# Softmax sums of a fused attention and feed-forward kernel: from TensorE to VectorE, with the transposes moved

## The chip, the cores and the metric

The kernel runs on one core of one Trainium2 chip. The metric is the device time of one execution in microseconds (us). Every experiment ran on the same chip as, and in turn with, the kernel before.

## The reference

Attention with normalised queries and keys, then a feed-forward layer with a squared ReLU, all in float32:

```python
q, k, v: (8, 12, 448, 64)          # batch, heads, sequence, head size
q_n = q / sqrt(mean(q*q, -1) + 1e-6) * g_q        # the same for k
attn = softmax(q_n @ k_n.T / 8)                   # 448 x 448 for each head
x = (attn @ v), rearranged to (3584, 768)
out = square(maximum(x @ w_in, 0)) @ w_out        # 768 -> 2048 -> 768
```

## The kernel before

Two heads make a pair, and there are 48 pairs. Twelve pairs make a span, and for each of the four spans a first product (`w_in`) and a second product (`w_out`) follow, each as seven block products in place of eight. The first twelve pairs run alone at the start. The other 36 are woven, twelve at a time, into the second product of spans 0 to 2. I call these three stretches the **stages**. In a stage TensorE alternates between a piece of second product (`ps`) and a piece of attention. The profiles show each matmul of the code as two records (`values()` issues eight for a pair, the trace has `pav` x16); counts of matmuls below are of records, save the 12.1 a pair in the prediction.

A pair of the stages, as `attention()` issued it before (each `yield` lets a piece of the second product in; cuts are marked):

```python
def attention(work, first):
    last = first + 2 * NPAIR
    for i in range(first, last + 1):
        if i + 3 < min(last + 2, B * NPAIR):
            load(i + 3)                    # q, k through SyncE's queue
        if i < last:
            scores(i, 0); scores(i, 1)     # TensorE sc, then ScalarE exp -> pr
        if i == first:
            yield
        if i > first:
            values(i - 1, False)           # TensorE pav (16), tot (4)
        if i < last:
            add_up(work, i, 1)             # VectorE acc = pr0 + pr1
            scores(i, 2); scores(i, 3)
        if i > first:
            finish(i - 1)                  # VectorE xT = pav * (1 / tot)
        yield
        if i < last:
            add_up(work, i, 2); add_up(work, i, 3)
        ...                                # combine_x(i - 1), load_v(i + 1)
        yield
        if i + 1 < last:
            transposes(i + 1)              # VectorE qk -> qkT
        if i + 2 < last:
            norm(i + 2)
        yield
```

The parts that matter below (line numbers in the profiles are of the kernel that was run: `acc` is L761 before and L760 after):

```python
def norm_by_squares(i):
    nc.scalar.activation(qkn..., raw..., AF.Square)                    # L707
    nc.vector.tensor_reduce(half, ..., AX, ALU.add)                    # L710
    ...                                                # L713 to L715, small
    nc.gpsimd.tensor_tensor(half, half, mhalf, ALU.pow)                # L716, 128x28
    for s in range(2):
        nc.gpsimd.tensor_tensor(qkn[:, s], raw[:, s], half..., ALU.mult)   # L718
    normed[i] = qkn

def transposes(i):
    ...
    for s in range(2):
        nc.vector.transpose(qkT[:, 0, s], qkn[:, s]...)                # L728
    nc.scalar.activation(qkT[:, 0, 0], qkT[:, 0, 0], AF.Copy, scale=gains[:, 0:1])   # L729

def values(i, pe_sums):
    pavs[i] = ps_o.tile([P, S], F32, tag="o", name="pav")              # one buffer in PSUM
    ...                                                                # 16 records
    sums(i, accs.pop(i), True, True)       # 4 records, with ones: sum over the keys, on all 64 rows

def finish(i):
    ...
    nc.vector.reciprocal(x, tot)           # 128x448
    nc.vector.tensor_tensor(x, pav, x, ALU.mult)
```

## Time and profile before

| | before |
|---|---|
| time, median | 1441.1 us (1440.99 to 1442.78, 3 runs) |
| profiled span | 1439.2 us |
| GpSimd's power L716, 36 times | mean 4813 ns |
| ScalarE's copy of qkT, waiting for VectorE's transposes | 174.0 us in all |
| VectorE's first sum, waiting for TensorE's tot | 122.3 us in all |

The busy shares, the stages and one pair's beat (the time from one pair to the next on TensorE) are shown in the prediction. In the profiles PE is TensorE, PEld its weight loads, DVE VectorE, ACT ScalarE, POOL GpSimd and SP SyncE; a q behind the name (SPq, ACTq) marks an instruction that issues a transfer. I cut the span at points of equal work: the first matmul of the first second product, then, in each stage, the start of the last 34 matmul records of the second product, which nothing interrupts. Stretch 1 is thus the start, 2 the first stage, 3 and 4 a first product and a stage each, and 5 the last products. This is the view of busy times by stretch; after the stretch and its length come PE, PEld, DVE, ACT and POOL busy with their instructions, the mean granted clock, the DMA share and GB/s.

```profile
0.00:275.43 275.43, 262.32 (x1022) 117.66 (x1022) 209.00 (x259) 200.78 (x307) 206.25 (x169) 0.99 0.79 252
275.43:479.21 203.78, 202.22 (x729) 87.13 (x727) 147.04 (x217) 58.55 (x73) 67.91 (x30) 1.00 0.46 98
479.21:822.68 343.47, 343.33 (x1106) 157.77 (x1105) 187.50 (x285) 83.28 (x115) 114.64 (x68) 1.00 0.41 97
822.68:1166.04 343.36, 343.24 (x1106) 157.78 (x1105) 188.18 (x285) 83.19 (x115) 113.79 (x68) 1.00 0.39 94
1166.04:1439.20 273.16, 265.53 (x706) 134.01 (x706) 72.64 (x117) 24.03 (x43) 31.52 (x32) 0.99 0.37 94
```

Subtract the second number from the first to read TensorE's idle time: 1.56 us in the first stage, 0.14 and 0.12 in the next two.

### The profile page before, as it was taken

How to read it: one execution, taken by the hardware profiler on the slowest of the kernel's cores; microseconds unless marked ns; L12 is line 12 of the kernel's file. 1: busy time of each engine (PE TensorE's matmuls, PEld its weight loads, DVE VectorE, ACT ScalarE, POOL GpSimd, SP SyncE). 2: the span in 40 equal slices, each digit the busy share in tenths (PEclk: the TensorE clock that was granted, in tenths of full speed). 3: DMA queues.
4: the chain of work that ended last, by engine and by line, in shares of the span. 5: the costliest groups of instructions: out<-in, count | busy, mean ns of one | idle time of the engine just before them, and what ended most of it. 6: DMA issues, size and time to landing. Idle time of an engine off the chain costs nothing.

```text
span 1439.2 us, 14368 instructions
## 1 busy us (share of the span) xinstructions
PE 1416.6 (98%) x4662; PEld 654.4 (45%) x4662; DVE 804.4 (56%) x1163; ACT 449.8 (31%) x652; POOL 534.1 (37%) x367
## 2 busy tenths in 40 slices
PE   7999999999999999999999999999999999999997
PEld 3433454444444455444444455544444445555553
DVE  6778888478767433456666633355666652332111
ACT  6887687423323012133232111223323201110000
POOL 5877688333442022523444012433334302221000
PEclk9999999999999999999999999999999999999999
DMA  8576898644445333344454342343544333333443
GB/s 236 171 219 162 301 383 315 180 87 107 101 89 102 97 88 88 97 98 106 98 109 88 89 102 87 93 115 81 109 98 103 76 83 87 87 88 102 106 113 70
DMA packets 423639, 180.37 MB, mean 125 GB/s; under 512 B 274820, under 2 KB 421508, under 8 KB 423556
## 3 DMA queue, kind: packets, MB, share of 16 engines
q1 hardware_dynamic: 419716, 178.91, 47.4%
q10 hardware_dynamic: 3712, 0.46, 0.2%
q8 instruction: 39, 0.64, 0.2%
q14 instruction: 44, 0.36, 0.1%
q0 software_dynamic: 128, 0.00, 0.0%
HBM read 146.28 MB, written 33.03 MB: 125 GB/s over the span
## 4 chain that ended last, share of the span: by engine, by line
PE 92%; DVE 4%; DMA 2%; issue 1%; ACT 1%; POOL 0%; SPq 0%; DVEq 0%; POOLq 0%; ACTq 0%
PE ps L973 32%; PE sc L748 11%; PE pav L772 10%; PE pd L926 10%; PE pa L926 10%; PE pc L926 10%; PE pb L926 5%; PE tot L783 4%; DVE acc L761 1%; DVE xT L796 1%; DMA sw<-w1s 1%; PE pt L734 1%; DMA words<-in_moe_w_out_dram 0%; ACT qkT L729 0%; DMA vt<-in_v_dram 0%
## 5 line engine op out<-in xcount | busy, mean ns | idle before, releaser
L716 POOL TENSOR_TENSOR half<-half,mhalf 128x28 f32<-128x28 f32 x36 | 173.3, 4813 | 343.1 <-DVE half L715 343.1
L973 PE MATMUL ps<-gT,sw 128*128 128x448 f32 x768 | 299.1, 542 | 0.0
L903 POOL TENSOR_TENSOR gT<-gT 128x448 f32<-128x448 f32 x96 | 94.9, 990 | 372.9 <-ACT gT L899 372.9
L973 PE MATMUL ps<-gC,sw 128*128 128x448 f32 x576 | 225.2, 542 | 0.0
L973 PEld LDWEIGHTS ps<-gT,sw 128*128 128x128 f32 x768 | 143.9, 190 | 149.9 <-issue 146.5
L748 PE MATMUL sc<-qkT 64*112 64x448 f32 x768 | 171.3, 564 | 6.4 <-ACT pr L753 3.8
L755 ACT ACTIVATE pr<-sc 112x896 f32<-112x896 f32 x120 | 104.7, 914 | 200.8 <-PE sc L748 200.8
L973 PEld LDWEIGHTS ps<-gC,sw 128*128 128x128 f32 x576 | 108.0, 190 | 112.3 <-issue 111.7
L926 PE MATMUL pa<-xT,sw 128*128 128x448 f32 x384 | 155.0, 540 | 0.8 <-DMA sw<-w1s 0.8
L772 PE MATMUL pav<-pr,vt 112*64 112x448 f32 x672 | 146.0, 549 | 1.3 <-PE sc L748 1.3
L899 ACT ACTIVATE gT<-gT 128x448 f32<-128x448 f32 x96 | 55.2, 575 | 285.7 <-DVE gT L941 285.6
L796 DVE RECIPROCAL xT<-tot 128x448 f32<-128x448 f32 x36 | 106.2, 2951 | 19.3 <-PE tot L783 19.3
L748 PEld LDWEIGHTS sc<-qkT 64*112 64x112 f32 x768 | 60.4, 173 | 105.5 <-issue 71.8
L926 PEld LDWEIGHTS pa<-xT,sw 128*128 128x128 f32 x384 | 72.8, 190 | 72.7 <-issue 72.2
L772 PEld LDWEIGHTS pav<-pr,vt 112*64 112x64 f32 x672 | 44.5, 137 | 89.3 <-issue 75.5
L926 PE MATMUL pd<-xT,sw 128*128 128x448 f32 x192 | 78.0, 542 | 0.6 <-DVE z L933 0.5
L729 ACT ACTIVATE qkT<-qkT,gains 128x448 f32<-128x448 f32 x36 | 24.1, 668 | 174.0 <-DVE qkT L728 174.0
L926 PE MATMUL pb<-xC,sw 128*128 128x448 f32 x192 | 77.7, 540 | 0.4 <-DVE xC L810 0.4
L926 PE MATMUL pc<-xC,sw 128*128 128x448 f32 x192 | 77.4, 539 | 0.0
L926 PE MATMUL pd<-xC,sw 128*128 128x448 f32 x192 | 77.4, 539 | 0.0
L926 PE MATMUL pc<-xT,sw 128*128 128x448 f32 x192 | 77.4, 539 | 0.0
L941 DVE TENSOR_TENSOR gT<-z,pd 128x448 f32<-128x448 f32 x32 | 19.9, 622 | 101.5 <-PE pd L926 101.4
(119 smaller groups left out, 1608.6 us busy)
## 6 DMA issues: line engine op xcount, KB each, us to landing
sw<-w1s SPq DMA_DIRECT2D x224, 192.0 KB, 2.4
sw<-w2s SPq DMA_DIRECT2D x168, 256.0 KB, 3.2
w1s<-gC SPq DMA_DIRECT2D x8, 1344.0 KB, 6.8
w2s<-gC SPq DMA_DIRECT2D x8, 1344.0 KB, 7.7
out_dram<-osb SPq DMA_DIRECT2D x184, 56.0 KB, 1.9
qk<-in_q_dram SPq DMA_DIRECT2D x144, 56.0 KB, 2.2
qk<-in_k_dram SPq DMA_DIRECT2D x144, 56.0 KB, 2.2
vt<-in_v_dram SPq DMA_DIRECT2D x72, 112.0 KB, 3.2
```

Source lines behind the costliest of these rows:

```text
L716: nc.gpsimd.tensor_tensor(half, half, mhalf, ALU.pow)
L729: nc.scalar.activation(qkT[:, 0, 0], qkT[:, 0, 0], AF.Copy, scale=gains[:, 0:1])
L748: nc.tensor.matmul(sc[:, h, 0:S], qkT[rows, at, 1, c * SP:(c + 1) * SP], qkT[rows, at, 0, :], start=True, stop=True)
L755: nc.scalar.activation(pr, sc[:, :, 0:S], AF.Exp)
L772: nc.tensor.matmul(pavs[i][h * D:(h + 1) * D, :], vs[i][:, h, c, :], pr[:, h, :], start=(c == 0), stop=(c == NJ - 1))
L783: nc.tensor.matmul(tots[i][h * D:(h + 1) * D, :], ones, pr[:, h, :], start=first, stop=last)
L796: nc.vector.reciprocal(x, tot)
L899: nc.scalar.activation(g, src, AF.Relu)
L903: nc.gpsimd.tensor_tensor(g, g, g, ALU.mult)
L926: nc.tensor.matmul(ps, stream[n + i][:, c], rhs[:, c], start=first and c == 0, stop=c == HC - 1, skip_group_check=not first)
L941: add(g, x, ps, ALU.add)
L973: nc.tensor.matmul(ps, stream[n][:, c % 4], rhs_of[i][:, c], start=c == 0, stop=c == HF - 1)
```

## The change

Its intent is to take the key sums (tot) off TensorE, which bounds the stages. VectorE already adds the four exponentials of a pair into `acc`. The remaining sum over 112 partitions is done by VectorE in squares of 32: transpose, reduce, add the four quarters, take the reciprocal of the small result (32x28), transpose back. The factors go out to DRAM (3.5 KB), and ScalarE's queue reads them back spread over 64 rows for each head. With tot gone, VectorE's order in a pair is rearranged so that the next pair's transposes come before the later sums. The start is rearranged too: the first piece of weight preparation comes after the first exponentials. Besides, a pair now lets the second product in at four points instead of three, SyncE's loads of q and k are issued in the third quarter of a pair, and every third result of the second product gets a PSUM buffer that tot used. The diff, cut to its core:

```diff
+    def fold(i):
+        acc, quarters = sums["acc"]..., sums["quarters"]
+        turned = places[NJ * (i + 1) % len(places)]...
+        nc.vector.transpose(turned, acc)
+        nc.vector.tensor_reduce(quarters[:, 0], turned..., AX, ALU.add)
+        for n in range(1, 4):
+            nc.vector.tensor_copy(quarters[0:32, n], quarters[n * 32:(n + 1) * 32, 0])
+        nc.vector.tensor_reduce(square[:, 0:2 * NG], quarters[0:32]..., AX, ALU.add)
+        nc.vector.reciprocal(square[:, 0:2 * NG], square[:, 0:2 * NG])
+        nc.vector.transpose(turned, square)
+    def spread(i):
+        for h in range(2):
+            nc.scalar.dma_start(xT[h * D:(h + 1) * D, b % 2, hp], sums["out"][i % 2]...to_broadcast([D, S]))
 ...
     def finish(i):
-            nc.vector.reciprocal(x, tot)
         nc.vector.tensor_tensor(x, pav, x, ALU.mult)
 ...                                     # attention_alone(), first pair
             if i:
                 combine_x(i - 1)
+            else:
+                yield                    # first weight piece here, behind norm(2)
 ...                                     # attention()
-            if i + 3 < min(last + 2, B * NPAIR):
-                load(i + 3)
             scores(i, 0); scores(i, 1)
             if i > first:
-                values(i - 1, False)
+                values(i - 1)
+                spread(i - 1)
             add_up(i, 1); scores(i, 2); scores(i, 3)
-            if i > first:
-                finish(i - 1)
             yield
+            if i + 1 < last:
+                transposes(i + 1)
             add_up(i, 2); add_up(i, 3)
-            combine_x(i - 1)
             load_v(i + 1)
             yield
-            if i + 1 < last:
-                transposes(i + 1)
+            fold(i)
+            finish(i - 1)
+            load(i + 3)
+            yield
+            nc.sync.dma_start(sums["out"][i % 2], sums["square"][0:2 * S // 32, 1])
+            combine_x(i - 1)
             norm(i + 2)
             yield
 ...                                     # second_product()
-            ps = ps_m.tile([P, S], F32, tag="m", name="ps")
+            ps = (ps_o.tile([P, S], F32, tag="t", name="ps") if j % 3 == 2
+                  else ps_m.tile([P, S], F32, tag="m", name="ps"))
```

More of the change, by code (lines that the diff above doesn't have):

```diff
@@ L455, in attention_then_ffn_bounded @@
     qk, qkT, ident, mhalf, gains, rstd0, _ = held
-    ones = consts.tile([SP, D], F32, name="ones")
     gT = consts.tile([P, NFC, 2 * S], F32, name="gT")
@@ L652, in attention_then_ffn_bounded @@
     pts = {}
-    vs, probs, pavs, tots, accs, normed, rstds = {}, {}, {}, {}, {}, {}, {0: rstd0}
+    vs, probs, pavs, tots, normed, rstds = {}, {}, {}, {}, {}, {0: rstd0}
     places = []
+    sums = {"out": [dram.tile([2 * S // 32, 32], F32, name=f"factors{n}") for n in range(2)]}
     def load(i):
@@ L749, in scores @@
                              start=True, stop=True)
-        pr = probs[i, c] = places[(NJ * i + c) % len(places)]
+        pr = probs[i, c] = places[(NJ * i + c) % len(places)][:SP]
         if i < NAT:
@@ L755, in scores, with add_up, sums_for, values @@
             nc.scalar.activation(pr, sc[:, :, 0:S], AF.Exp)
-    def add_up(work, i, c):
-        if c == 1:
-            accs[i] = work.tile([SP, 2, S], F32, tag="acc", name="acc", bufs=1)
-        nc.vector.tensor_tensor(accs[i], probs[i, 0] if c == 1 else accs[i], probs[i, c], ALU.add)
+    def add_up(i, c):
+        acc = sums["acc"][:SP]
+        nc.vector.tensor_tensor(acc, probs[i, 0] if c == 1 else acc, probs[i, c], ALU.add)
+    def fold(i):
+        NG = S // 32
+        acc, quarters = sums["acc"].rearrange("p h q -> p (h q)"), sums["quarters"]
+        turned = places[NJ * (i + 1) % len(places)].rearrange("p h q -> p (h q)")
+        nc.vector.transpose(turned, acc)
+        nc.vector.tensor_reduce(quarters[:, 0], turned.rearrange("p (n k) -> p n k", k=32), AX, ALU.add)
+        for n in range(1, 4):
+            nc.vector.tensor_copy(quarters[0:32, n], quarters[n * 32:(n + 1) * 32, 0])
+        square, turned = sums["square"][:, 0], sums["square"][:, 1]
+        nc.vector.tensor_reduce(square[:, 0:2 * NG], quarters[0:32].rearrange("p a n -> p n a"), AX, ALU.add)
+        nc.vector.reciprocal(square[:, 0:2 * NG], square[:, 0:2 * NG])
+        nc.vector.transpose(turned, square)
+    def spread(i):
+        b, hp = divmod(i, NPAIR)
+        for h in range(2):
+            nc.scalar.dma_start(xT[h * D:(h + 1) * D, b % 2, hp],
+                              sums["out"][i % 2].rearrange("(h g) t -> h () (g t)", h=2)[h].to_broadcast([D, S]))
+    def sums_for(work):
+        sums["acc"] = work.tile([P, 2, S], F32, tag="acc", name="acc", bufs=1)
+        sums["quarters"] = work.tile([P, 4, 2 * S // 32], F32, tag="quarters", name="quarters", bufs=1)
+        sums["square"] = work.tile([32, 2, 32], F32, tag="square", name="square", bufs=1)
+        nc.gpsimd.memset(sums["acc"][96:P], 0.0)
+        nc.gpsimd.memset(sums["square"][:, 0], 1.0)
     def places_for(work, n):
-        places[:] = [work.tile([SP, 2, S], F32, tag=f"pr{m}", name="pr", bufs=1) for m in range(n)]
-    def values(i, pe_sums):
+        places[:] = [work.tile([P, 2, S], F32, tag=f"pr{m}", name="pr", bufs=1) for m in range(n)]
+    def values(i):
         pavs[i] = ps_o.tile([P, S], F32, tag="o", name="pav")
+        if i < NAT:
+            tots[i] = ps_o.tile([P, S], F32, tag="t", name="tot")
         for c in range(NJ):
@@ L773, in values @@
                                  start=(c == 0), stop=(c == NJ - 1))
-            if pe_sums:
-                sums(i, pr, c == 0, c == NJ - 1)
-        if not pe_sums:
-            sums(i, accs.pop(i), True, True)
-    def sums(i, pr, first, last):
-        if first:
-            tots[i] = ps_o.tile([P, S], F32, tag="t", name="tot")
-        for h in range(2):
-            nc.tensor.matmul(tots[i][h * D:(h + 1) * D, :], ones, pr[:, h, :], start=first, stop=last)
+            for h in range(2 if i < NAT else 0):
+                nc.tensor.matmul(tots[i][h * D:(h + 1) * D, :], sums["ones"], pr[:, h, :],
+                                 start=(c == 0), stop=(c == NJ - 1))
     def finish(i):
         b, hp = divmod(i, NPAIR)
-        tot, pav = tots.pop(i), pavs.pop(i)
+        pav = pavs.pop(i)
         x = xT[:, b % 2, hp]
         if i < NAT:
+            tot = tots.pop(i)
             nc.vector.reciprocal(x.rearrange("d (p j) -> d j p", j=NJ), tot.rearrange("d (j p) -> d j p", j=NJ))
@@ L794, in finish @@
             pav = pav.rearrange("d (j p) -> d p j", j=NJ)
-        else:
-            nc.vector.reciprocal(x, tot)
         nc.vector.tensor_tensor(x, pav, x, ALU.mult)
@@ L836, in attention_alone @@
             yield
-            values(i, True)
+            values(i)
             finish(i)
@@ L842, in attention_alone, with attention @@
                 load(i + 3)
-    def attention(work, first):
+    def attention(first):
         last = first + 2 * NPAIR
         for i in range(first, last + 1):
-            if i + 3 < min(last + 2, B * NPAIR):
-                load(i + 3)
             if i < last:
@@ L856, in attention @@
             if i > first:
-                values(i - 1, False)
+                values(i - 1)
+                spread(i - 1)
             if i < last:
-                add_up(work, i, 1)
+                add_up(i, 1)
                 scores(i, 2)
                 scores(i, 3)
-            if i > first:
-                finish(i - 1)
             yield
+            if i + 1 < last:
+                transposes(i + 1)
             if i < last:
-                add_up(work, i, 2)
-                add_up(work, i, 3)
-            if i > first:
-                combine_x(i - 1)
+                add_up(i, 2)
+                add_up(i, 3)
             if i < min(last, B * NPAIR - 1):
@@ L872, in attention @@
             yield
-            if i + 1 < last:
-                transposes(i + 1)
+            if i < last:
+                fold(i)
+            if i > first:
+                finish(i - 1)
+            if i + 3 < min(last + 2, B * NPAIR):
+                load(i + 3)
+            yield
+            if i < last:
+                nc.sync.dma_start(sums["out"][i % 2], sums["square"][0:2 * S // 32, 1])
+            if i > first:
+                combine_x(i - 1)
             if i + 2 < last:
@@ L909, in first_product @@
             add = nc.vector.tensor_tensor
-            sums = {}
+            ps_of = {}
             for i in range(7):
@@ L914, in first_product @@
                              A12: ("pa", B21), A22: ("pd", T4), S4: ("pc", B22)}[i]
-                first = into not in sums
+                first = into not in ps_of
                 if first and into == "pa":
                     if span == 0 and f:
-                        sums[into] = ps_o.tile([P, S], F32, tag="ot"[f % 2], name="pa")
+                        ps_of[into] = ps_o.tile([P, S], F32, tag="ot"[f % 2], name="pa")
                     else:
-                        sums[into] = ps_s.tile([P, 2, 512], F32, tag="s", name="pa")[:, 0, 0:S]
+                        ps_of[into] = ps_s.tile([P, 2, 512], F32, tag="s", name="pa")[:, 0, 0:S]
                 elif first:
-                    sums[into] = ps_m.tile([P, S], F32, tag="m", name=into)
-                ps = sums[into]
+                    ps_of[into] = ps_m.tile([P, S], F32, tag="m", name=into)
+                ps = ps_of[into]
                 load_blocks(n + i + 5)
@@ L1004, in attention_then_ffn_bounded @@
     nc.vector.memset(clamp2, 255.0 * 2.0 ** 23)
-    nc.vector.memset(ones, 1.0)
     def ahead(u, nxt):
@@ L1024, in attention_then_ffn_bounded @@
             places_for(work, NJ)
-            weights(4)
-            for u, _ in enumerate(attention_alone()):
-                weights(min(EARLY, 8 + (EARLY - 8) * (u + 1) // (NAT - 1)))
+            sums["ones"] = work.tile([SP, D], F32, tag="ones", name="ones", bufs=1)
+            nc.vector.memset(sums["ones"], 1.0)
+            for u, _ in enumerate(attention_alone(), -1):
+                weights(min(EARLY, 8 + (EARLY - 8) * (u + 1) // (NAT - 1)) if u >= 0 else 4)
                 if u == NAT - 2:
@@ L1055, in attention_then_ffn_bounded @@
                 places_for(work, NJ + 1)
-                places.append(qkT[:SP, 1])
+                places.append(qkT[:, 1])
+                sums_for(work)
                 total, done = HC * (7 * HF + 4) - 20, 0
-                for u, _ in enumerate(attention(work, nxt)):
-                    while done < min(total, total * (u + 1) // (6 * NPAIR + 1)):
+                for u, _ in enumerate(attention(nxt)):
+                    while done < min(total, total * (u + 1) // (8 * NPAIR + 1)):
                         next(rest)
```

## The prediction

> **What bounds the kernel now.** I read the page's busy shares first, then the groups, the waits, the chain in order of time and the timeline of one pair. The busy shares of the page:
>
> ```profile
> PE 1416.6 (98%) x4662; PEld 654.4 (45%) x4662; DVE 804.4 (56%) x1163; ACT 449.8 (31%) x652; POOL 534.1 (37%) x367
> ```
>
> TensorE sits idle for 22.6 us of 1439.2 in all. The stretches show where: busy times in the three stages in which twelve pairs of attention are woven into a second product (273-492, 619-836, 962-1179 us), then in the last second product, which stands alone.
>
> ```profile
> 273.00:492.20 219.20, 217.64 (x772) 94.51 (x771) 155.91 (x228) 59.88 (x75) 69.41 (x32) 1.00 0.45 97
> ...
> 619.00:835.70 216.70, 216.58 (x769) 94.31 (x770) 140.69 (x201) 59.06 (x73) 70.66 (x32) 1.00 0.45 97
> ...
> 962.00:1179.00 217.00, 216.88 (x770) 94.41 (x770) 140.72 (x200) 59.06 (x73) 70.65 (x32) 1.00 0.42 92
> ```
>
> After span and the name of each column come PE, PEld, DVE, ACT and POOL busy. TensorE idles 1.56 us in the first stage and 0.12 us in each of the others, so it alone sets the beat there. The chain in order of time gives one pair's beat:
>
> ```profile
> 997.04 3.16 PE pav L772 x16
> 1000.20 0.75 PE tot L783 x4
> 1000.95 1.69 PE sc L748 x8
> 1002.64 9.22 PE ps L973 x24
> 1011.86 1.69 PE sc L748 x8
> ```
>
> These five add to 16.51 us. The piece that the change removes is the 0.75 us of tot. Now the same pair on VectorE and GpSimd, from the timeline:
>
> ```profile
> 1001.07 1.09 DVE L761 TENSOR_TENSOR acc<-pr 112x896 f32<-112x896 f32 x1 [4.35 <-PE tot L783]
> 1002.08 2.95 DVE L796 RECIPROCAL xT<-tot 128x448 f32<-128x448 f32 x1
> ...
> 1008.89 1.13 DVE L728 STREAM_TRANSPOSE qkT<-qk 128x448 f32<-128x448 f32 x2
> 1011.07 1.08 DVE L710 TENSOR_REDUCE half<-qk 128x28 f32<-128x896 f32 x1 [1.05 <-ACT qk L707]
> 1012.19 0.78 DVE L713 COPY other<-half 32x28 f32<-32x28 f32 x4
> ```
>
> ```profile
> 1013.49 4.79 POOL L716 TENSOR_TENSOR half<-half,mhalf 128x28 f32<-128x28 f32 x1 [9.63 <-DVE half L715]
> 1018.36 2.01 POOL L718 TENSOR_TENSOR qk<-qk,half 128x448 f32<-128x448 f32 x2
> ```
>
> The reader is to see the round trip: VectorE's norm sums (L710 to L715, 2.33 us) start GpSimd's power and two products (6.9 us), and the next pair's transposes (L728) need those products. Before, the transposes are the last thing but the norm in a pair's VectorE work, so the 6.9 us lie beside some 9 us of sums, reciprocal and products: the products end at 1020.4, the transposes start at 1025.2.
>
> **What the Trainium skill says.** "TensorE: Matmul & The Clock Gate", Part 3, says that narrow matmuls can run concurrently in column tiles. The trace agrees: four tot records of 539 ns each take 0.75 us together. So the saving is 0.75 us a pair, not four times 0.54. "VectorE: DVE Perf Modes", "First, the fixed hardware budget", says the reciprocal is an iterative divide with a repeat count of 8; the trace has 2951 ns for 448 columns beside 625 ns for a product of that shape, 4.7 times. The same page, "The three transpose paths", says VectorE transposes only inside 32x32 blocks, which is why the new sum needs quarters added and a second transpose. "DMA: Bandwidth & Descriptors", "Anatomy of one DMA", puts the fixed cost of a transfer at about 2 us; the page's issues agree (56 KB of output land in 1.9 us, 56 KB of q in 2.2).
>
> **The change, part by part.** It touches the 36 pairs from number 12 on; the first twelve keep sums on TensorE.
>
> Removed on TensorE: 36 x 0.753 = 27.1 us, all of it on the path.
>
> Removed on VectorE: one wide reciprocal, 2.95 us a pair. Added: a transpose of 896 columns (twice a 448 one, whose step in the timeline is 0.56: 1.1), a reduce as L710 (1.1), three 32-row copies (0.2 each), a short reduce (0.2), a reciprocal of 28 columns (28/448 of 2.95 plus some 0.06: 0.25), a 32x32 transpose (0.15); with waits of 0.1 between dependent ones about 3.5 us. As busy time that is +0.5 us a pair, to 12.2 of 15.8: no bound by itself.
>
> Added transfers: 3.5 KB out, 224 KB back. At some 2 us and 2.5 us each, and 8 MB in all against 180 MB, they fit. The write is issued in the last quarter of pair i, the read after the next pair's first two exponentials, and the product needs it in the third quarter: about 7 us of slack.
>
> Moved: VectorE's order becomes first sum, transposes, two sums, fold, product with the factors, norm. I took this from the instruction order of the changed kernel: between a norm and the next transposes stands just one sum of 1.1 us, now and then an addition of 0.6. So GpSimd's 6.9 us, hidden before, now stand in a loop with nearly all of VectorE's work. One turn, from the end of the transposes: two sums 2.24, fold 3.5, product 0.55, norm 2.33, GpSimd 0.08 + 4.8 + 2.04, last transpose 0.6: 16.2 us, and 1.55 other operations (output additions, output transposes, combinations) of 0.58 a pair that the order puts inside the loop: 17.1 us. TensorE's new beat is 16.57 - 0.75 = 15.8 (16.57 being the mean that 12.1 second-product matmuls a pair give). The loop is 1.3 us longer than the beat.
>
> How much shows: the product (xT) frees the one PSUM tile that the next pair's pav needs. From the first pair's first scores its transposes end at 7.0 (four scores of 0.85, three matmuls between, two transposes), its norm at 7.0 + 2.24 + 3.5 + 2.33 = 15.1, the second transposes at 15.1 + 6.9 + 0.6 = 22.6, and the product at 22.6 + 2.24 + 0.6 + 3.5 + 0.55 = 29.5. TensorE wants it at 15.1 (first pair, without pav) + 15.8 + 1.7 (two scores) = 32.6, so it comes 3.1 early. Nine further turns make 11.7 us of lateness, so 8.6 us of stall by that count; going through the twelve pairs one by one with the same durations gives 6.7, as two short turns regain something. The first such stage has, besides, four groups of four combinations (L887 to L891, 0.6 each) inside the loop: 9.6 us more; pair by pair, 18.4. The same going through, done for the order before, gives 0.7 us in the first stage and none later, against 1.56 and 0.12 in the trace. Stalls together: 18.4 + 6.7 + 6.7 = 31.8 us.
>
> Given back: the first stage's 1.6 us of idle time, whose chain (tot, sum, reciprocal, transposes, qkT) is cut. At the start the first weight piece now comes after the first exponentials, which in the trace start at 16.1 us though scores are there at 10.7; but the transfers for weights are then queued later while the DMA engines are full (300 GB/s between 8 and 28 us), and the second pair's pav still waits for VectorE: I count 1 us. The third PSUM buffer for the second product gains nothing; TensorE does not wait there (126.57 busy of the last 134.2, the rest being the tail).
>
> Sum: 1441.1 - 27.1 - 1.6 - 1.0 + 31.8 = 1443.
>
> **Rivals.**
> (a) TensorE stays the bound and all of the saving comes: 1441.1 - 29.7 = 1411 to 1414. For it: 98% busy, VectorE idle 44%. Against it: the loop above; it would have to be 1.3 us a pair shorter. If the fold takes 3.0 instead of 3.5, stalls come to 16 and the time to 1428.
> (b) The transfers through DRAM come late: ScalarE's queue is in order, so a read that waits for its factors holds up the exponentials behind it. For it: the write waits for a VectorE that lags. Against it: some 7 us of slack. If each pair lost 2 us more, 1443 + 72 = 1515.
> (c) The clock gate: the page named first, "The HAM clock gate", has the clock halved after about 3.4 us of idleness. The trace shows a grant of 0.50 from 16 to 22 us, after TensorE was nearly idle from 10.7 to 17. My gaps in the first stage are 5 to 6 us twice; each could cost another 3 us: up to 1450. In later stages gaps of 1.4 us are too short.
>
> **Range and chances.** The loop's excess is a small difference of large terms: 0.5 us in one turn is worth about 13 us over three stages. From a fold of 3.0 without throttling to one of 4.0 with it gives 1422 to 1461, which I give 8 in 10. Beyond it, 2% faster (below 1412.3) needs no stall at all: 0.07. 2% slower (above 1469.9) needs rival (b) or loops of over 18 us: 0.07. Within 2%: 0.86.
>
> **What would show it.** Tot of 112x448 from acc is gone, TensorE's busy time 27 us less. VectorE's waits show the transposes waiting for GpSimd's products some 5 us a pair, where before they waited for none. TensorE waits for the product (xT) before pav, mostly in 273-492. The stages that last 219 and twice 217 us now last about 227 (219.2 - 1.6 - 9.0 + 18.4) and twice 215 (217.0 - 9.0 + 6.7). Wrong would be: no wait of transposes on GpSimd (then rival a), exponentials or products waiting for DMA (then b), a mean clock well under 1.0 in these stages (then c).

## The result, and the profile after

The changed kernel took 1453.66 us (median of 4 runs, 1450.64 to 1454.43), the kernel before beside it 1441.05 (1439.98 to 1442.78). The ratio is 1.0082, 95% interval 1.0065 to 1.01: within 2%, and inside the predicted range, but 10.7 us above the predicted 1443. Here and below, a ratio is the mean time of one kernel's fast runs over the mean of the other's fast runs in the same rounds, so it is not quite the ratio of the medians quoted.

The busy shares of the page after:

```profile
PE 1401.0 (97%) x4518; PEld 647.2 (45%) x4518; DVE 824.3 (57%) x1415; ACT 449.1 (31%) x652; POOL 532.7 (37%) x373
```

The 144 tot matmuls are gone (4662 to 4518), yet TensorE is only 15.6 us less busy, not 27.1. The stretches after, cut at the same points of work, show why:

```profile
0.00:279.76 279.76, 265.10 (x1022) 119.04 (x1023) 211.21 (x259) 200.58 (x307) 206.47 (x170) 0.99 0.77 248
279.76:493.28 213.52, 199.60 (x681) 85.04 (x679) 156.18 (x302) 58.77 (x73) 68.32 (x31) 0.97 0.48 106
493.28:836.11 342.83, 334.60 (x1057) 154.48 (x1057) 193.63 (x369) 82.98 (x115) 113.19 (x70) 1.00 0.44 105
836.11:1178.80 342.69, 336.15 (x1058) 154.68 (x1057) 193.57 (x369) 82.76 (x115) 113.19 (x70) 1.00 0.42 102
1178.80:1451.50 272.70, 265.53 (x706) 134.00 (x706) 69.70 (x116) 24.04 (x43) 31.52 (x32) 0.99 0.37 94
```

Set beside the stretches before, with tot's 9.03 us for each stage (12 x 0.753) taken from busy time:

| stretch | longer by | of it TensorE idle | of it matmuls slower | forecast |
|---|---|---|---|---|
| start | +4.33 | +1.55 | +2.78 | -1.0 |
| first stage | +9.74 | +12.36 | +6.41 | +7.8 |
| second | -0.64 | +8.09 | +0.30 | -2.3 |
| third | -0.67 | +6.42 | +1.94 | -2.3 |
| end | -0.46 | -0.46 | 0.00 | 0 |
| sum | +12.3 | +27.96 | +11.43 | +2.2 |

The sum of the two middle columns less 27.1 is the first. In the stages 26.87 us of the 27.09 that TensorE saved came back as idle time, and another 8.65 us as matmuls that ran slower; the start adds 4.33.

What TensorE waits for, and what VectorE waits for, is in the view of waits (after the colon: us in all, times, longest us):

```profile
DVE qkT L728 <- POOL qk L718: 87.0, 49, 5.7
ACT qkT L729 <- DVE qkT L728: 52.8, 24, 4.0
PEld pav L802 <- DVE xT L819: 43.9, 22, 6.0
PE pav L802 <- DVE xT L819: 28.0, 17, 5.2
...
ACT pr L755 <- DMA xT<-factors: 25.0, 7, 4.6
```

Before, the first of these did not exist, and the second was 174.0 us. TensorE now waits 28.0 us for VectorE's product xT, because that product frees the PSUM tile in which the next pav is made. One turn of VectorE in the second stage, from the timeline (start, us, engine, line, operation, out<-in, count, and in brackets the idle time before with its releaser):

```profile
705.42 0.65 DVE L728 STREAM_TRANSPOSE qkT<-qk 128x448 f32<-128x448 f32 x1 [4.40 <-POOL qk L718]
706.33 0.65 DVE L728 STREAM_TRANSPOSE qkT<-qk 128x448 f32<-128x448 f32 x1 [0.25 <-POOL qk L718]
706.89 2.25 DVE L760 TENSOR_TENSOR acc<-acc,pr 112x896 f32<-112x896 f32 x2
...
709.59 1.10 DVE L768 STREAM_TRANSPOSE pr<-acc 128x896 f32<-128x896 f32 x1
...
713.15 0.20 DVE L775 STREAM_TRANSPOSE square<-square 32x32 f32<-32x32 f32 x1
713.29 0.57 DVE L819 TENSOR_TENSOR xT<-pav,xT 128x448 f32<-128x448 f32 x1
713.78 1.06 DVE L710 TENSOR_REDUCE half<-qk 128x28 f32<-128x896 f32 x1
...
722.02 0.65 DVE L728 STREAM_TRANSPOSE qkT<-qk 128x448 f32<-128x448 f32 x1 [4.40 <-POOL qk L718]
722.92 0.65 DVE L728 STREAM_TRANSPOSE qkT<-qk 128x448 f32<-128x448 f32 x1 [0.25 <-POOL qk L718]
```

and GpSimd in the same turn:

```profile
716.17 4.80 POOL L716 TENSOR_TENSOR half<-half,mhalf 128x28 f32<-128x28 f32 x1 [9.88 <-DVE half L715]
721.05 1.84 POOL L718 TENSOR_TENSOR qk<-qk,half 128x448 f32<-128x448 f32 x2
```

This is the loop of the prediction. VectorE comes to the transposes 4.40 us too early, GpSimd waits 9.88 us for VectorE's norm, and each waits for the other once a turn. The turn takes 722.02 - 705.42 = 16.60 us. TensorE would need 15.75: its score groups for these two pairs begin at 712.37 and 728.12, before it stalls. So VectorE falls 0.85 us behind in this turn, and TensorE stands 1.17 us at the next pair's pav. This turn isn't an exception: from the second pair's transposes to the twelfth's (639.93 to 809.98 in the second stage, 982.72 to 1153.36 in the third) ten turns take 17.0 and 17.1 us each on average. In the first stage, where the output of the first product is combined as well, the stall is longer. TensorE's timeline there:

```profile
325.38 1.76 PE L748 MATMUL sc<-qkT 64*112 64x448 f32 x8
332.37 4.75 PE L802 MATMUL pav<-pr,vt 112*64 112x448 f32 x12 [5.23 <-DVE xT L819]
336.90 1.50 PE L802 MATMUL pav<-qkT,vt 112*64 112x448 f32 x4
```

After 5.23 us of idleness, sixteen pav matmuls take 5.96 us (332.37 to 338.33, where the next scores begin); the undisturbed sixteen, as in the prediction's chain, take 3.16. The stretches on both sides of that point have these granted clocks (the number after POOL's):

```profile
320.00:332.00 12.00, 7.15 (x23) 3.10 (x21) 9.85 (x18) 3.67 (x5) 2.27 (x3) 0.97 0.31 60
332.00:346.00 14.00, 13.63 (x40) 5.49 (x41) 10.36 (x19) 3.33 (x5) 6.94 (x3) 0.78 0.45 109
```

Cut finer, the grant is 0.50 from 331.22 to 338.05. The stall is thus paid twice: as idle time, and as a slow clock behind it.

**The start.** The first exponentials come earlier, as intended, but what follows them is later. ScalarE before:

```profile
14.29 0.94 ACT L593 ACTIVATE gC<-gC,clamp 128x768 f32<-128x768 uint32 x1 [4.21 <-DVE gC L580]
16.09 2.19 ACT L753 ACTIVATE pr<-sc,rstd 112x448 f32<-112x448 f32 x4
...
19.17 1.16 ACT L753 ACTIVATE pr<-sc,rstd 112x448 f32<-112x448 f32 x2
```

and after:

```profile
9.98 2.21 ACT L753 ACTIVATE pr<-sc,rstd 112x448 f32<-112x448 f32 x4
...
16.50 1.06 ACT L693 ACTIVATE qk<-qk 112x1024 f32<-112x1024 f32 x1 [4.32 <-DMA qk<-in_k_dram]
...
19.52 0.94 ACT L592 ACTIVATE gC<-gC,clamp 128x768 f32<-128x768 uint32 x1 [1.96 <-DVE gC L579]
...
21.33 2.19 ACT L753 ACTIVATE pr<-sc,rstd 112x448 f32<-112x448 f32 x4
```

The first exponentials move from 16.09 to 9.98. But the norm of the third pair (L693) is ahead of the weight piece (L592) in ScalarE's order, and it waits for q and k until 16.50. The weight piece goes from 14.29 to 19.52 and stands ahead of the next exponentials, which go from 19.17 to 21.33.

### The profile page after: what moved, and what is told of

Read it like the earlier page. It is cut to its first block, busy times and chain, and to the rows that moved or that the text cites. A ratio compares the mean times of both kernels' runs of the same rounds, so it can differ in the third digit from the quotient of the medians.

```text
span 1451.5 us, 14567 instructions
## 1 busy us (share of the span) xinstructions
PE 1401.0 (97%) x4518; PEld 647.2 (45%) x4518; DVE 824.3 (57%) x1415; ACT 449.1 (31%) x652; POOL 532.7 (37%) x373
## 4 chain that ended last, share of the span: by engine, by line
PE 69%; issue 16%; DVE 6%; DMA 4%; POOL 2%; SPq 1%; ACT 1%; ACTq 0%; POOLq 0%; DVEq 0%
PE ps L1004 20%; PE pd L956 10%; PE pc L956 9%; PE pa L956 9%; PE pav L802 7%; PE sc L748 6%; PE pb L956 4%; PE tot L805 2%; POOL qk L718 2%; DVE acc L760 1%; DMA sw<-w2s 1%; DMA factors<-square 1%; DVE quarters L769 1%; DVE pr L768 1%; DMA sw<-w1s 1%
## 5 line engine op out<-in xcount | busy, mean ns | idle before, releaser
L716 POOL TENSOR_TENSOR half<-half,mhalf 128x28 f32<-128x28 f32 x36 | 176.4, 4899 | 357.2 <-DVE half L715 317.8
L802 PE MATMUL pav<-pr,vt 112*64 112x448 f32 x672 | 154.5, 573 | 33.4 <-DVE xT L819 28.0
L728 DVE STREAM_TRANSPOSE qkT<-qk 128x448 f32<-128x448 f32 x72 | 45.2, 639 | 94.3 <-POOL qk L718 87.0
L760 DVE TENSOR_TENSOR acc<-acc,pr 112x896 f32<-112x896 f32 x60 | 64.2, 1070 | 16.8 <-ACT pr L755 14.3
```

What stands on the lines that cost most here:

```text
L728: nc.vector.transpose(qkT[:, 0, s], qkn[:, s].rearrange("p g e -> p (g e)"))
L760: nc.vector.tensor_tensor(acc, probs[i, 0] if c == 1 else acc, probs[i, c], ALU.add)
L802: nc.tensor.matmul(pavs[i][h * D:(h + 1) * D, :], vs[i][:, h, c, :], pr[:, h, :], start=(c == 0), stop=(c == NJ - 1))
```

## The experiments

All results are correct unless marked. Times are medians.

| run | time | ratio to before (95%) |
|---|---|---|
| e1_tr_behind_sums | 1434.9 | 0.9954 (0.9938 to 0.9971) |
| e2_tr_last | 1500.75 | 1.0412 (1.0394 to 1.0429) |
| e3_pow_as_product (wrong) | 1416.71 | 0.9832 (0.9815 to 0.9848) |
| e4_const_factors (wrong) | 1453.38 | 1.0087 (1.0071 to 1.0104) |
| e5_spread_late | 1423.41 | 0.9868 (0.9853 to 0.9883) |
| e6_spread_late_head | 1418.95 | 0.984 (0.9825 to 0.9855) |
| e7_head_old | 1450.24 | 1.0051 (1.0037 to 1.0064) |
| e8_before_order | 1439.89 | 0.998 (0.9965 to 0.9996) |
| e9_two_buffers | 1419.3 | 0.9852 (0.9836 to 0.9869) |
| e10_write_first | 1420.69 | 0.9852 (0.9833 to 0.9872) |

The theory is the loop through GpSimd. The rivals are the trip through DRAM (which also makes transposes and products late, by way of ScalarE's queue), the order of VectorE's work by itself, and the start.

**e3_pow_as_product: one link of the loop shortened.** Its output is wrong, which doesn't matter for the time.

```diff
-        nc.gpsimd.tensor_tensor(half, half, mhalf, ALU.pow)
+        nc.gpsimd.tensor_tensor(half, half, mhalf, ALU.mult)
```

> Wrong result on purpose: in the norm of pairs 12 to 47 GpSimd's power is replaced by a product of the same operands, some 0.2 us in place of 4.8, all orders and waits as in the changed kernel. Loop theory: a turn falls by 4.6 us to about 12.6, far under the beat; all stalls of the three stages go: about 208 to 210, 207 and 207 us, 1418 to 1424 in all. If VectorE's work or the DRAM trip is the cause: 1450 or more.

Measured: 1416.71 us. The same 36 instructions fell from a mean of 4899 ns to 349:

```profile
L716 POOL TENSOR_TENSOR half<-half,mhalf 128x28 f32<-128x28 f32 x36 | 12.6, 349 | 440.0 <-DVE half L715 406.5 <-ACT pr L755 20.5 <-DMA out_dram<-osb 13.0
```

VectorE's transposes wait 0.3 us in all for GpSimd, and TensorE waits 2.0 us for xT. The three stages are 9.5, 8.8 and 8.2 us shorter than before: the 9.03 of tot almost whole. With the transfers, the fold and VectorE's order as in the change, the length of the power alone decides whether the saving shows. The loop is confirmed. This run also settles what has no run of its own: the fourth point at which the second product is let in and the later loads of q and k are in it as well, so together they cost no more than the 0.2 to 0.8 us by which two of its stages miss 9.03.

**e4_const_factors: no dependence on the trip through DRAM.** The spread reads constants written once at the start, so it never waits for a pair's factors. Its output is wrong, which doesn't matter for the time.

```diff
-                              sums["out"][i % 2]...to_broadcast([D, S]))
+                              sums["const"]...to_broadcast([D, S]))
```

> Wrong result on purpose: the factors are still written to DRAM each pair, but the spread reads a constant in DRAM that was written once at the start, so ScalarE's queue and the product no longer wait for the write. Loop theory: within 5 us of the changed kernel (1449 to 1454). If the DRAM trip in ScalarE's in-order queue is what costs (exponentials wait 25 us in all behind the spread): 1425 to 1435.

Measured: 1453.38 us, ratio 1.0087 against 1.0082 for the change. VectorE's wait for GpSimd is 88.2 us. The 25.0 us that exponentials in the change stand behind a spread cost nothing, since the loop is longer anyway. The rival falls for the changed kernel.

**e8_before_order: the order by itself.** In the kernel before, the transposes go to the start of the second quarter, as in the change, with tot kept.

```diff
             yield
+            if i + 1 < last:
+                transposes(i + 1)
             if i < last:
                 add_up(work, i, 2)
 ...
-            if i + 1 < last:
-                transposes(i + 1)
             if i + 2 < last:
                 norm(i + 2)
```

> The kernel before with the order of the change alone: transposes at the start of the second quarter, ahead of the two later sums, the norm staying last; sums over keys still on TensorE. The reciprocal and the product then stand between norm and transposes, beside GpSimd's 7 us, so a turn is two sums 2.25, norm 2.33, GpSimd 7.0, transpose 0.6, some other operations: about 13 us, under the beat of 16.57. Loop theory: no harm from the order alone, 1438 to 1442. If the order is bad in itself: slower by 10 us or more.

Measured: 1439.89 us, 0.2% below before. So the moved transposes do no harm by themselves. By the terms of the prediction the loop without fold and product is 0.6 + 2.24 + 2.33 + 6.92 = 12.1 us (an estimate), well below the beat of 16.5. It takes the order and the fold together to make it too long.

**e7_head_old: the start of before.**

```diff
             if i:
                 combine_x(i - 1)
-            else:
-                yield
 ...
+            weights(4)
-            for u, _ in enumerate(attention_alone(), -1):
+            for u, _ in enumerate(attention_alone()):
```

> The changed kernel with the start of the kernel before: first weight piece ahead of the attention. In the traces the first product ended 4.3 us later in the changed kernel (4.3, 5.7, 2.8 and 4.7 us in it, e1, e2 and e4 with the same start, 0.1 in e3), where I had forecast 1 us earlier. If the new start is what costs, 3 to 5 us less than the changed kernel: 1448 to 1451, a ratio of 1.005 to 1.007. If the start only varies from run to run, or the delay comes from elsewhere: 1453, 1.008.

Measured: 1450.24 us against 1453.66 for the change, though from different rounds. The ratios are 1.0051 (1.0037 to 1.0064) and 1.0082 (1.0065 to 1.01), intervals that just miss each other. So the new start costs 3.4 us by the medians and 4.5 by the ratios. Not all of the 4.33 us in the profiles is thereby explained: the profiled run of e7 reached the first second product at 278.19 us, against 275.43 before with the same start. That point varied by about 3 us among profiled runs with the old start, and from 275.5 to 281.2 among those with the new one. I leave it open.

**e2_tr_last: the transposes back at their old place.** They go from ahead of the sums to just ahead of the norm, so that GpSimd's work lies beside other work again.

```diff
             yield
-            if i + 1 < last:
-                transposes(i + 1)
             add_up(i, 2); add_up(i, 3)
 ...
             combine_x(i - 1)
+            if i + 1 < last:
+                transposes(i + 1)
             norm(i + 2)
```

> The changed kernel with the transposes back at their place of before, just ahead of the norm, so behind the sums, the fold and the product. The loop through GpSimd is then gone (its 7 us lie beside sums and fold), but the transposes now end a chain in one pair: scores, pav, scores, exponentials, last sum, fold 3.75, product 0.6, transposes 1.1, qkT 0.7, which I count at 16 to 17 us against 15.8. Loop theory: no wait of the transposes on GpSimd, scores wait for qkT instead, time 1440 to 1458, so about no gain. If the DRAM trip were the cause: also no gain, but with pav still waiting for the product. If the order plays no part: 1453.

Measured: 1500.75 us, a miss by over 40 us. VectorE indeed waits no longer for GpSimd, but now TensorE waits for the transposes (`sc` for ScalarE's copy of qkT: 60.6 us on TensorE, 82.7 on its weight loads). VectorE in one pair:

```profile
738.39 1.29 DVE L760 TENSOR_TENSOR acc<-acc,qkT 112x896 f32<-112x896 f32 x1 [0.46 <-DVE acc L760]
742.03 0.62 DVE L1021 TENSOR_TENSOR ct<-y,ps 128x448 f32<-128x448 f32 x1 [2.35 <-PE ps L1004]
...
743.10 1.10 DVE L768 STREAM_TRANSPOSE pr<-acc 128x896 f32<-128x896 f32 x1
...
747.31 1.15 DVE L728 STREAM_TRANSPOSE qkT<-qk 128x448 f32<-128x448 f32 x2
```

and TensorE:

```profile
729.93 1.76 PE L748 MATMUL sc<-qkT 64*112 64x448 f32 x8
...
748.69 3.23 PE L748 MATMUL sc<-qkT 64*112 64x448 f32 x8 [2.94 <-ACT qkT L729]
```

From one pair's first scores to the next's are 18.76 us. This is another loop, without GpSimd: the transposes stand behind the fold and product (743.10 to 747.31, 4.2 us), and these behind output additions that wait 2.35 us for a second-product piece. I had counted this chain at 16 to 17 us; the wait of the output additions, which stand ahead of the fold in VectorE's order, was not in that count. Nor was the clock: for the same 4518 matmuls TensorE's busy time is 1419.6 us here and 1401.0 in the change, so 18.6 of the 48.7 us by which this span is longer are slower matmuls. Before, the place was harmless: neither fold nor product stood between the last sum and the transposes there.

**e1_tr_behind_sums: in between.** The transposes go behind the two later sums, but ahead of the fold. GpSimd's work then has the first sum and the two others beside it, and the fold does not delay the scores.

```diff
             yield
-            if i + 1 < last:
-                transposes(i + 1)
             add_up(i, 2); add_up(i, 3)
+            if i + 1 < last:
+                transposes(i + 1)
```

> The changed kernel with one move: each pair's transposes stand behind the two later sums instead of ahead of them, still ahead of the fold. If the loop through GpSimd is the cause (transposes, sums, fold, product, norm, GpSimd's power and products, next transposes), the two sums (2.25 us a pair) now lie beside GpSimd's 7 us and one turn falls from some 17.2 us to about 15, under TensorE's beat of 15.8: the second and third woven stages go from 216 us to about 208 each, the first from 228 to some 215, together about 28 us less, so 1424 to 1430 us. If the transfer through DRAM sets the pace, or VectorE's mere amount of work, nothing of that changes: 1450 or more.

Measured: 1434.9 us, faster than both kernels but 5 us short of what I expected. VectorE's wait for GpSimd fell from 87.0 to 11.8 us. The next bound is the rival that the loop had hidden. ScalarE in one pair of e1:

```profile
752.13 1.72 ACT L755 ACTIVATE pr<-sc 112x896 f32<-112x896 f32 x2 [1.79 <-PE sc L748]
760.20 1.10 ACTq L780 DMA_DIRECT2D xT<-factors  x2
761.41 0.92 ACT L755 ACTIVATE pr<-sc 112x896 f32<-112x896 f32 x1 [7.55 <-issue]
```

and SyncE's queue:

```profile
752.49 2.13 SPq L666 DMA_DIRECT2D qk<-in_q_dram  x4
754.72 1.99 SPq L666 DMA_DIRECT2D qk<-in_k_dram  x4
756.80 0.52 SPq L647 DMA_DIRECT2D sw<-w2s  x1
757.42 0.55 SPq L902 DMA_DIRECT2D factors<-square  x1
```

VectorE finished the factors at 753.5, but their write is issued at 757.42, behind eight loads. The spread waits for it until 760.20, and the exponentials behind it in ScalarE's order follow at 761.41.

**e5_spread_late: e1 with the spread behind the later exponentials.** The queue is left as it is; only ScalarE's order changes.

```diff
                 values(i - 1)
-                spread(i - 1)
             if i < last:
                 add_up(i, 1)
                 scores(i, 2)
                 scores(i, 3)
+            if i > first:
+                spread(i - 1)
             yield
```

> The kernel of e1 (transposes behind the sums) with the two reads of the spread issued on ScalarE after the third and fourth score instead of after the second. In e1 exponentials still waited behind the spread: in one pair the write of the factors was issued 3.9 us after they were ready, since the eight loads of q and k stood ahead of it in its queue, and the exponentials followed only 4 us after their scores. With the loop through GpSimd out of the way, this DRAM trip in an in-order queue should be the next cost: if so 1424 to 1430, against 1434.9 for e1. If it still hides, or the product now waits for the later read instead: 1433 to 1437.

Measured: 1423.41 us, just below the expected range and 11.5 us less than e1 (in other rounds, but the intervals of their ratios do not overlap). In e1, then, the trip through DRAM was on the path.

**e6_spread_late_head: e5 with the weight piece ahead of the third norm.** The first exponentials still come first, then the first weight piece, then norm(2), which has to wait for q and k.

```diff
             scores(i, 0)
             scores(i, 1)
+            if not i:
+                yield
             if i + 2 < NAT:
                 norm(i + 2)
 ...
             if i:
                 combine_x(i - 1)
-            else:
-                yield
```

> The kernel of e5 with one move at the start: the first piece of weight work is emitted right behind the first two exponentials but ahead of the norm of the third pair, whose q and k come late. The start then has both: exponentials at 10 us instead of 16, and weight work on VectorE not behind a wait for that transfer. If the start of the changed kernel is late because of that wait, 3 to 6 us less than e5; if it is late for another cause (weight transfers queued behind q and k), the same as e5.

Measured: 1418.95 us, 4.5 less than e5. On ScalarE the exponentials come at 9.99, the weight piece at 14.20, the norm at 16.46 and the next exponentials at 17.43, all earlier than in the kernel before, the weight piece by 0.09 us only. This is the fastest correct version found, 1.6% below before and 2.4% below the change. Its first stage is 199.68 us (203.78 before), its later stretches 335.51 and 335.47 (343.47 and 343.36).

One cost grew on the way. GpSimd in a pair of e6:

```profile
698.98 2.69 POOL L718 TENSOR_TENSOR qk<-qk,half 128x448 f32<-128x448 f32 x2
```

and VectorE beside it:

```profile
699.28 1.59 DVE L760 TENSOR_TENSOR acc<-acc,pr 112x896 f32<-112x896 f32 x1 [2.93 <-ACT pr L755]
700.97 1.65 DVE L760 TENSOR_TENSOR acc<-acc,qkT 112x896 f32<-112x896 f32 x1
```

In the change, where VectorE stood still at that time, the two products took 1.84 us and a sum about 1.1. Where they run at the same time, both slow down by about half. In e3 it is the first sum that falls beside the products: of its two groups one then takes 1.63 us (mean of twelve), while the later sums stay at 1.07 to 1.09.

**e9_two_buffers: e6 without the third PSUM buffer of the second product.**

```diff
-            ps = (ps_o.tile([P, S], F32, tag="t", name="ps") if j % 3 == 2
-                  else ps_m.tile([P, S], F32, tag="m", name="ps"))
+            ps = ps_m.tile([P, S], F32, tag="m", name="ps")
```

> The fastest version so far (pieces reordered, spread late, head in order; 1418.95 us), with the second product's results in the two PSUM tiles of before instead of three. The prediction held that the third tile gains nothing, as TensorE does not wait for a free tile there. If so: within 2 us of 1419, that is 1416 to 1421, and a last stage (its second product alone) no longer than before. If, on the contrary, part of the gain comes from the third tile: 1422 or more, with TensorE waiting ahead of ps for VectorE's or ScalarE's reads.

Measured: 1419.3 us against 1418.95, ratios 0.9852 and 0.984 with overlapping intervals. The third buffer gains nothing, as predicted.

**e10_write_first: e6 with the factors' write ahead of the q and k loads.**

```diff
             if i > first:
                 finish(i - 1)
+            if i < last:
+                nc.sync.dma_start(sums["out"][i % 2], sums["square"][0:2 * S // 32, 1])
             if i + 3 < min(last + 2, B * NPAIR):
                 load(i + 3)
             yield
-            if i < last:
-                nc.sync.dma_start(sums["out"][i % 2], sums["square"][0:2 * S // 32, 1])
```

> The fastest version so far with the factors' write issued right behind the fold, ahead of the eight q/k loads that SyncE's queue issues at that point. If the trip through DRAM still costs something there (ScalarE waited 16.9 us in all for the spread ahead of its copies of qkT), the wait goes and 0 to 4 us come off: 1415 to 1419. Against it: the write waits for the fold, and the loads of q, k and weight blocks now stand behind that wait in SyncE's queue; if that matters the time rises above 1421.

Measured: 1420.69 us, ratio 0.9852 (0.9833 to 0.9872) against 0.984: no gain. ScalarE's copies of qkT wait 7.2 us for the spread instead of 16.9, but SyncE's queue now waits 141.6 us for the fold (28.7 in e6), with the loads behind it. After e5 the write's place is off the path.

## Why the prediction was right or wrong

**The removal** of tot: right. It is 9.03 us in each stage, and e3 shows stages 9.5, 8.8 and 8.2 us shorter when nothing stands in the way.

**The loop through GpSimd**: right, in mechanism and nearly in length. The turn shown above, from the end of one pair's transposes (706.98) to the end of the next's (723.57), has: two sums 2.25 (forecast 2.24), one other addition 0.53 (0.58 each), fold with its waits 3.76 (3.5), product 0.50 (0.55), norm 2.31 (2.33), GpSimd with its gaps 6.80 (6.92), last transpose 0.65 (0.6). Without the other addition and with 0.2 of overlaps taken off, this is some 16.1 where the forecast had 16.2 (its own terms add to 16.14). That is so close because the fold's 0.26 too little is made up by the overlaps and by 0.12 too much for GpSimd. With the other operations a mean turn was forecast at 17.1 us; the ten turns of the later stages average 17.0 and 17.1. TensorE's beat was forecast at 15.8, and in e3, where TensorE hardly waits, the score groups of ten pairs of the second stage come 15.84 us apart. VectorE's wait before the transposes was forecast as some 5 us a pair. It is 4.40 + 0.25 in the turn shown, but on average only 2.4 (87.0 us over 36 pairs): in some turns VectorE waits ahead of the transposes for something else, as at 738.46, where an output addition had waited 3.70 us for a second-product piece, and the transposes behind it then waited 0.08 and 0.25.

**The stall that comes of it**: right in the later stages, differently made up in the first. TensorE's idle time is 8.23 and 6.54 us in the second and third stage's stretch (forecast 6.7 each), and 13.92 in the first (18.4).

**The clock**: the term that was set to zero. The prediction had it as rival (c), with up to 7 us in the first stage, and left it out of the sum. It came in beside the stall: matmuls in the stages ran 6.41 + 0.30 + 1.94 = 8.65 us slower, nearly all of it after gaps. With 2.78 us more at the start, that is why TensorE's busy time fell by 15.6 us, not by the 27 given as a sign. In the first stage idle and slowed time together are 13.92 + 6.41 = 20.3 us where 18.4 of idle time was forecast, so two errors of 4.5 and 6.4 us there nearly hid each other. The prediction also held that gaps of 1.4 us in the later stages were too short for the clock. After the gaps of 1.0 to 1.5 us there the trace indeed shows no lower grant; what it had wrong is their length. Each later stage has one gap of 2.2 us: after the one in the third stage (2.17 us, ending at 1142.55) the grant was 0.50 from 1143.60 to 1147.01, which is most of the 1.94 us, after the one in the second (2.20 us, ending at 799.70) it stayed at 1.00.

**The start**: wrong in sign, and the largest error. The step "I count 1 us" of gain became a loss: +4.33 us in the profiles, 3.4 to 4.5 us by e7. I had looked only at what the moved exponentials gain and at the weight transfers. I had not asked what stands between: the third pair's norm, issued ahead of the weight piece, waits for q and k and keeps both ScalarE's weight piece and the exponentials behind it back. e6, which swaps these two, gets it back (4.5 us).

**The trip through DRAM**, rival (b): rightly given little weight for this kernel (e4), but it was hidden, not absent. In e1 it became the bound and was worth 11.5 us (e5). The forecast of "some 7 us of slack" overlooked that SyncE's queue issues eight loads ahead of the write. It also took some 2 and 2.5 us for the two transfers. The section "Anatomy of one DMA" behind the 2 us is on transfers issued by GpSimd; these are issued by SyncE and ScalarE, and took 2.71 and 2.73 us in the chain (see the last section).

**Rival (a)**, the whole saving at 1411 to 1414: not what came. It is what e3 and e6 approach from two sides (1416.7 and 1418.95), by cutting the loop at the power, or at the order with two more repairs.

**The third buffer**: right (e9).

Term by term the errors add up: start 5.3, first stage 1.9, second 1.7, third 1.6, end -0.5: 10.0 of the 10.1 us by which the profiles' difference (12.3) exceeds the forecast's (2.2).

What stays open: why GpSimd's power took 5.57 us in four of the 36 turns, two of them in the first stage, and 4.80 in most; and the variation of about 3 us at the start.

## What to carry to other kernels

When work leaves the bounding engine, do not only check that the receiving engine has idle share left. Follow one turn of its order, through every engine that it waits for, and compare that length with the new, shorter beat. Where an instruction stands in an in-order engine or queue decides which loop it lengthens: the same two transposes, at three places in an otherwise unchanged kernel, gave 1434.9, 1453.7 and 1500.8 us. When one loop is cut, look again for the next one behind it before judging the idea.

## What the Trainium skill lacked or had wrong

- "GPSIMD Engine Reference", sections 1 and 3.1: section 3.1 times an addition but no power. Here a power of 128x28 on GpSimd took 4.8 to 4.9 us and a product of the same shape 0.35 us. Section 1 says that its SBUF interfaces are shared with VectorE and contended by instructions with two SBUF inputs. The runs agree, and have a size, which that section does not give: where sums of 112x896 and products of 128x448 fell together, a sum took 1.59 to 1.65 us instead of 1.1, and two products 2.69 us instead of 1.84.
- "TensorE: Matmul & The Clock Gate", Part 1, has the half rate come after at least one idle window of about 3.4 us. The gap of 5.23 us agrees. But shorter gaps had it behind them too (a gap is from the modelled end of one matmul to the start of the next): 2.20 us in the first stage (ending at 457.03, grant 0.50 from 457.52 to 460.93) and 2.17 us in the third (ending at 1142.55, grant 0.50 from 1143.60 to 1147.01); one of 2.20 us in the second had not. Gaps of 1.5 us or less in the stages had none. In all, 17 waits for xT, 28.0 us, came with 8.65 us of slower matmuls in the stages.
- No page has the time of a small write to DRAM with a read that waits for it. In the chain of the changed kernel, writing 3.5 KB took 2.71 us and the spread of it 2.73 us, both without the queue's time ahead of them, so a trip of 5.4 us, where the prediction had taken some 2 and 2.5.
